# Attention of batches 2 to 4 inside a matmul stream: visits of three groups in place of two

## The chip, the cores and the metric

The kernel runs on one core of a Trainium2 chip. The metric is the device time of one execution in microseconds (us), the median of three timed runs. One more execution was profiled; it has a time and a trace of its own.

## What is computed

Windowed attention over four batches, then two feed-forward blocks over all 2304 tokens. In the reference, cut to what matters here:

```python
# q, k, v: (4, 8, 576, 64)
scores = scale * q @ k.T                       # 32 keys back; heads 4-7 with a stride of 4
scores = where(mask, scores, -1e9); scores -= max(scores)
attn = exp(scores); attn /= attn.sum() + 1e-9
x = (attn @ v).transpose(0, 2, 1, 3).reshape(2304, 512)
x = ((x @ w_a) * (x @ w_b)) @ w_out            # 512 -> 1536 -> 512
h = x @ w_in                                   # 512 -> 2048
out = (max(h, 0) + alpha * min(h, 0)) @ w_out2 # 2048 -> 512
```

## The kernel before

**The big matmuls.** Every large product is made of three matmuls of float32r data (high part times high, high times low, low times high). Tokens lie along the free axis. The first three token tiles, of 512 tokens each, take 37 **steps** each: for each of the 12 slices `f` of the hidden axis a step for product `pa`, a step for `pb`, and a step that expands the slice before into the four accumulators `accA` (lines 519 to 521), 12 matmuls of 128x512 in each step. Between them VectorE multiplies `g = pa*pb` (line 853, the "gate product") and ScalarE and VectorE split it into parts (line 282 and 279). After the third tile come the last 768 tokens and the second block, which the change doesn't touch in its code.

**Attention.** A **group** is two heads by three query windows of 64; a batch has 12 groups. Batch 1 is done ahead of the first tile. Batches 2, 3 and 4 are woven into tiles 1, 2 and 3, in **visits**. A group passes through these methods of `Group`:

- `scores` (line 378): six float32 matmuls of 64x64 by 96 columns. Each occupies a quarter of the array; the trace shows each float32 matmul as two records, so a group has 12.
- `largest` (393, VectorE): mask and row maximum, "maxima"; `exps` (407, ScalarE): three exponentials with their sums; `weigh` (414 to 418, VectorE): divides by the sums.
- `transposed` (430): three transposes through TensorE, one record each; `moved` (435, ScalarE): copies them out of PSUM as `pt`.
- `values` (443): six matmuls of 96x64 by 64 columns, 12 records; `placed` (477, VectorE): copies into the token tile.

A visit (`visit_scores`) issues the value products of the two groups of the visit before, and the scores of two new ones, ahead of one step's matmuls; `visit_turn` transposes both new groups together three steps later. A batch is 7 visits: the first has scores alone, the last values alone, five have both. The times of visits in steps come from `slots` (about 2.25, 2.64 and 2.3 steps a group in the three tiles).

**Order.** `at_step(before, k, fn)` and `at_step(after, k, fn)` hang work ahead of or behind the matmuls of step `k`; `behind` comes last in a step. What is not pinned by `keep_in_program_order` a scheduler may move by its own estimate of times. `convey` advances jobs that convert weights (read from `in_w2`, written to `wsd`). All DMAs go through SyncE's queue. `reload_o` fetches the output weights of slice `f` for tiles 2 and 3 (`wof`, `wod`). `load_qk(n + 3)` and `load_v(n + 3)` ask for the data of the group after next-but-one as soon as group `n` has used its place; there are three places for each.

Of the kernel before, what the change touches and what calls it, by code (L numbers as in the profile page):

```python
# [25 lines left out]
QT = 64  # L26
# [4 lines left out]
GS = 3  # L31
KS = GS * QT + WINDOW
# [33 lines left out]
def tile_kernel(ctx: ExitStack, tc: tile.TileContext, qk, v, mask, wab, wo1, w2, alpha, out):  # L66
# [57 lines left out]
    st_ring = Ring(ft, a0 + 2400, GS * KT, 2)  # L124
    et_ring = Ring(ft, a0 + 2976, GS * KT, 3)
    pt_ring = Ring(ft, a0 + 3840, GS * 2 * QT, 2)
    sm_ring = Ring(ft, a0 + 4608, 3 * GS, 4)
    mk = cut(ft, a0 + 4648, 720).bitcast(BF16).rearrange("p (m k) -> p m k", m=5)
# [13 lines left out]
    nal = cut(ft, a0 + 5376, NFB)  # L142
# [6 lines left out]
    held = [start_of[t] + x for t in (2, 3) for x in (-2, -1, 0, 1)]  # L149
# [199 lines left out]
    class Group:  # L349


        def __init__(self, b, i):
# [3 lines left out]
            self.swap = 0  # L356
            self.shared = None
# [5 lines left out]
        def scores(self):  # L363
            Group.scores_of([self])

        @staticmethod
        def scores_of(groups):


            for a, group in enumerate(groups):  # L370
                group.swap = a
                group.tq = tqs.pop(group.n)
                group.sp = group.psum(0, "sp") if group.shared is None else group.shared
            for s in range(GS):
                for group in groups:
                    for j in range(2):
                        half, to = (slice(x * 64, (x + 1) * 64) for x in (j, j ^ group.swap))
                        nc.tensor.matmul(
                            group.sp[to, s * KT:(s + 1) * KT],
                            lhsT=group.tq[half, s * QT:(s + 1) * QT],  # L380
                            rhs=group.tq[half, GS * QT + s * QT:GS * QT + s * QT + KT],
                            start=True, stop=True,
                        )
            for group in groups:
                if group.b:
                    at_step(after, now[0] + 1, lambda n=group.n + 3: behind.append(lambda: load_qk(n)))

        def largest(self, then=None):
            then = then.weights() if then else iter(())
            self.st = st_ring.next().rearrange("p (s k) -> p s k", k=KT)  # L390
            self.sm = sm_ring.next().rearrange("p (a s) -> p a s", s=GS)
            for s in range(GS):
                ins = nc.vector.tensor_tensor_reduce(  # L393
                    out=self.st[:, s], in0=self.sp[:, s * KT:(s + 1) * KT],
# [4 lines left out]
                if self.n in (NC * NG, NC * NG + 1) and s == 0:  # L399
# [4 lines left out]
        def exps(self):  # L404
            self.et = et_ring.next().rearrange("p (s k) -> p s k", k=KT)
            for s in range(GS):
                nc.scalar.activation(  # L407
                    self.et[:, s], self.st[:, s], AF.Exp, bias=self.sm[:, 0, s:s + 1], scale=-1.0, accum_out=self.sm[:, 1, s:s + 1]
                )
            self.st = None  # L410
# [27 lines left out]
        def values(self):  # L438
            tv = tvs.pop(self.n)
            self.ap = self.psum(2, "ap") if self.shared is None else self.shared[:, GS * KT:]  # L440
            for s in range(GS):
                for j in range(2):
                    nc.tensor.matmul(
                        self.ap[j * 64:(j + 1) * 64, s * QT:(s + 1) * QT],
                        lhsT=tv[:, s, j], rhs=self.pt[:, s, j ^ self.swap],
# [3 lines left out]
            if self.b:  # L449
                at_step(after, now[0] + 1, lambda n=self.n + 3: behind.append(lambda: load_v(n)))  # L450
# [819 lines left out]
```

## Time and profile before

| what | value |
|---|---|
| median of three runs | 865.87 us (865.82 to 866.27) |
| profiled execution, its own time | 865.0 us |
| its span in the trace | 863.2 us, 1.8 us less than its time |
| busy: TensorE, VectorE, ScalarE | 855.7, 626.7, 538.9 us |
| mean granted TensorE clock | 0.999 of full speed |

The span runs from the first to the last instruction of the trace. TensorE's busy time counts overlapping matmuls once; a matmul's own duration is longer than the distance to the next one, so costs are read from starts, not from durations. A visit is read from the start of the last large matmul ahead of it to the start of the second large matmul behind it.

### The profile page before, as it was taken

The numbers are of one execution on the slowest core, as the hardware profiler recorded it, in microseconds if no ns is written. First come the engines' busy times: TensorE is split into PE (matmuls) and PEld (weight loads), VectorE is DVE, ScalarE is ACT, GpSimd is POOL, SyncE is SP. The second block draws the span as 40 slices with busy tenths as digits, with TensorE's granted clock in tenths as the row PEclk, the third lists the DMA queues.
The fourth block names the chain that finished last, engine by engine and source line by source line (L and its number), as shares of the span: only waits on it lengthen the run. The fifth ranks groups of instructions, "written<-read, shape, count | busy, mean of one in ns | idle before, by whom it ended". The sixth has DMA issues, their size and how long they took to land.

```text
span 863.2 us, 15630 instructions
## 1 busy us (share of the span) xinstructions
PE 855.7 (99%) x5416; PEld 779.1 (90%) x5416; DVE 626.7 (73%) x1450; ACT 538.9 (62%) x1195; POOL 0.7 (0%) x6
## 2 busy tenths in 40 slices
PE   9999999999999999999999999999999999999998
PEld 5688887888878888899999999999999999999998
DVE  5788675567676678789796837997567896567954
ACT  7998874556655667655544537785566755665542
POOL 0000000000000000000000000000000000000000
PEclk9999999999999999999999999999999999999999
DMA  9999864589899898989555659788888887778875
GB/s 263 332 327 314 284 244 152 198 274 312 268 319 320 286 319 288 323 310 320 201 189 192 217 178 321 252 251 261 269 258 254 250 265 221 231 247 259 268 223 184
DMA packets 108126, 225.28 MB, mean 261 GB/s; under 512 B 12305, under 2 KB 27409, under 8 KB 108049
## 3 DMA queue, kind: packets, MB, share of 16 engines
q1 hardware_dynamic: 108048, 224.30, 79.2%
q8 instruction: 43, 0.70, 0.3%
q14 instruction: 35, 0.28, 0.1%
HBM read 169.72 MB, written 54.53 MB: 260 GB/s over the span
## 4 chain that ended last, share of the span: by engine, by line
PE 83%; DMA 8%; DVE 4%; ACT 4%; issue 1%; SPq 0%; ACTq 0%; DVEq 0%
PE acc L1179 20%; PE at L874 12%; PE pb L874 8%; PE pa L874 8%; DMA wsd<-rt 4%; PE accA L519 4%; PE accA L521 4%; PE accA L520 4%; PE pa L519 3%; PE pb L519 3%; PE pa L521 3%; PE pa L520 3%; PE pb L520 3%; PE pb L521 3%; DMA ft<-in_w 2%; PE tp L430 1%
## 5 line engine op out<-in xcount | busy, mean ns | idle before, releaser
L1179 PE MATMUL acc<-rt 128*128 128x384 f32 x1008 | 187.2, 334 | 0.0
L1179 PEld LDWEIGHTS acc<-rt 128*128 128x128 f32 x1008 | 175.8, 188 | 0.4 <-ACT ft L1162 0.4
L282 DVE TENSOR_TENSOR rt<-ft,rt 128x512 fp32r<-128x512 f32 (+3 forms) x165 | 116.3, 709 | 60.2 <-ACT rt L279 59.4
L279 ACT CAST rt<-ft 128x512 fp32r<-128x512 f32 (+3 forms) x165 | 103.6, 636 | 84.9 <-DMA wsd<-rt 20.4
L890 ACT COPY ft<-at 128x384 f32<-128x384 f32 x105 | 50.0, 476 | 53.6 <-PE at L874 52.6
L874 PE MATMUL at<-rt 128*128 128x384 f32 x414 | 83.4, 335 | 0.0
L874 PEld LDWEIGHTS at<-rt 128*128 128x128 f32 x414 | 72.6, 188 | 0.5 <-ACT ft L890 0.5
L519 PE MATMUL accA<-rt 128*128 128x512 f32 (+1 forms) x160 | 62.9, 393 | 0.2 <-ACT rt L279 0.2
L520 PE MATMUL accA<-rt 128*128 128x512 f32 (+1 forms) x160 | 61.7, 386 | 0.2 <-DVE rt L282 0.2
L521 PE MATMUL accA<-rt 128*128 128x512 f32 (+1 forms) x160 | 61.2, 385 | 0.1
L196 DVE SCALAR_TENSOR_TENSOR ft<-ft 128x512 uint32<-128x512 uint32 x60 | 41.2, 686 | 27.3 <-ACT ft L193 21.0
L407 ACT ACTIVATE ft<-ft 128x96 f32<-128x96 f32 x144 | 52.1, 365 | 12.0 <-DVE ft L393 11.9
L282 DVE TENSOR_TENSOR rt<-gx,rt 128x768 fp32r<-128x768 f32 x43 | 41.1, 956 | 21.5 <-ACT rt L279 21.1
L874 PE MATMUL pb<-rt 128*128 128x384 f32 x276 | 55.6, 336 | 0.0
L874 PE MATMUL pa<-rt 128*128 128x384 f32 x276 | 55.2, 334 | 0.0
L874 PEld LDWEIGHTS pb<-rt 128*128 128x128 f32 x276 | 48.3, 188 | 0.5
L279 ACT CAST rt<-gx 128x768 fp32r<-128x768 f32 x43 | 36.0, 836 | 20.4 <-PE acc L1179 18.8
L874 PEld LDWEIGHTS pa<-rt 128*128 128x128 f32 x276 | 48.5, 188 | 0.0
L193 ACT ACTIVATE ft<-ft 128x512 uint32<-128x512 uint32 x60 | 40.4, 673 | 12.3 <-DMA ft<-in_w 12.1
L190 ACT ACTIVATE ft<-ft 128x512 f32<-128x512 f32 x60 | 40.1, 670 | 10.9 <-DMA ft<-in_w 6.9
L874 PE MATMUL at<-rt,rx 128*128 128x384 f32 x216 | 43.9, 337 | 0.2 <-ACT ft L890 0.2
L874 PEld LDWEIGHTS at<-rt,rx 128*128 128x128 f32 x216 | 37.8, 188 | 1.2 <-ACT ft L890 1.2
(157 smaller groups left out, 1755.3 us busy)
## 6 DMA issues: line engine op xcount, KB each, us to landing
rt<-wsd SPq DMA_DIRECT2D x318, 256.0 KB, 3.2
wsd<-rt SPq DMA_DIRECT2D x112, 256.0 KB, 4.7
ft<-in_w SPq DMA_DIRECT2D x32, 512.0 KB, 5.8
ft<-in_qk SPq DMA_DIRECT2D x48, 208.0 KB, 5.0
ft<-in_wab SPq DMA_DIRECT2D x19, 512.0 KB, 6.4
rt<-wod SPq DMA_DIRECT2D x19, 512.0 KB, 5.1
rx<-wod SPq DMA_DIRECT2D x17, 512.0 KB, 4.5
ft<-in_v SPq DMA_DIRECT2D x48, 144.0 KB, 5.1
```

The source lines that it names most:

```text
L190: held(nc.scalar.activation(f, high.bitcast(F32), AF.Prelu, scale=2.0 ** -112, alpha=-2.0 ** 32))
L193: nc.scalar.activation(low, low, AF.Copy, scale=0.933 * 2.0 ** -29)
L196: nc.vector.scalar_tensor_tensor(out=fi, in0=fi, scalar=3, in1=low, op0=ALU.logical_shift_left, op1=ALU.bitwise_or)
L279: hi_eng.copy(hi, x)
L282: lo_eng.tensor_tensor(out=lo, in0=x, in1=hi.bitcast(F32), op=ALU.subtract)
L407: nc.scalar.activation(self.et[:, s], self.st[:, s], AF.Exp, bias=self.sm[:, 0, s:s + 1], scale=-1.0, accum_out=self.sm[:, 1, s:s + 1])
L519: nc.tensor.matmul(acc, lhsT=wh, rhs=rh, start=first, stop=False)
L520: nc.tensor.matmul(acc, lhsT=wh, rhs=rl, start=False, stop=False)
L521: nc.tensor.matmul(acc, lhsT=wl, rhs=rh, start=False, stop=last)
L874: nc.tensor.matmul(acc[:, :HT], lhsT=a, rhs=x[:, b, c], start=start and c == k == 0, stop=c == 1 and k == 2, skip_group_check=not start,)
L890: nc.scalar.copy(out, acc[:, :HT])
L1179: nc.tensor.matmul(acc[a][:, :HT], lhsT=u, rhs=q[:, b, i % 2], start=new and first and k == 0, stop=last and k == 2, skip_group_check=not new,
```

## The change

Visits of batches 2 to 4 now handle three groups (`VISIT`), so a batch has 5 visits, one every 6 steps, from step 8 of tile 1 and step 5 of tiles 2 and 3 (the scores of the very first stand three steps earlier). Each group is transposed alone, in steps 3, 4 and 5 behind its visit. Nine score windows alternate between two PSUM banks; the values of the groups go to the bank `pa`, which the product `pa` also uses, and the last window to the end of a score bank. Scores are kept in program order. Maxima and exponentials share their places, which leaves room for three `pt`. Maxima are queued behind all else of the visit's step, the gate product too. The loads of queries and keys follow in steps 1, 2 and 3 behind the visit, those of values in steps 2, 3 and 4. `reload_o` asks one step sooner and splits where it did. One more step, three ahead of tile 3, goes without `convey`.

```diff
 GS = 3
+VISIT, VISITS_AT = 3, (8, 5, 5)
...
-    st_ring = Ring(ft, a0 + 2400, GS * KT, 2)
-    et_ring = Ring(ft, a0 + 2976, GS * KT, 3)
-    pt_ring = Ring(ft, a0 + 3840, GS * 2 * QT, 2)
-    sm_ring = Ring(ft, a0 + 4608, 3 * GS, 4)
+    et_ring = Ring(ft, a0 + 2400, GS * KT, 4)
+    pt_ring = Ring(ft, a0 + 3552, GS * 2 * QT, 3)
+    sm_ring = Ring(ft, a0 + 4704, 3 * GS, 6)
...
-    held = [start_of[t] + x for t in (2, 3) for x in (-2, -1, 0, 1)]
+    held = [start_of[t] + x for t in (2, 3) for x in (-2, -1, 0, 1)] + [start_of[2] - 3]
...
-            at_step(after, k + 2, lambda: split(hi, lo, lo.bitcast(F32), nc.scalar, nc.vector))
-            at_step(after, k + 4, lambda: tc.keep_in_program_order(nc.sync.dma_start(out=wod[f], in_=w.bitcast(F32))))
+            at_step(after, k + 3, lambda: split(hi, lo, lo.bitcast(F32), nc.scalar, nc.vector))
+            at_step(after, k + 5, lambda: tc.keep_in_program_order(nc.sync.dma_start(out=wod[f], in_=w.bitcast(F32))))
...
-        def scores_of(groups):
-
-
-            for a, group in enumerate(groups):
-                group.swap = a
-                group.tq = tqs.pop(group.n)
-                group.sp = group.psum(0, "sp") if group.shared is None else group.shared
+            if not self.sp:
+                bank = self.psum(0, "sp")
+                self.sp = [bank[:, s * KT:(s + 1) * KT] for s in range(GS)]
+            tq = tqs.pop(self.n)
             for s in range(GS):
-                for group in groups:
-                    for j in range(2):
-                        half, to = (slice(x * 64, (x + 1) * 64) for x in (j, j ^ group.swap))
-                        nc.tensor.matmul(
-                            group.sp[to, s * KT:(s + 1) * KT],
-                            lhsT=group.tq[half, s * QT:(s + 1) * QT],
-                            rhs=group.tq[half, GS * QT + s * QT:GS * QT + s * QT + KT],
-                            start=True, stop=True,
-                        )
-            for group in groups:
-                if group.b:
-                    at_step(after, now[0] + 1, lambda n=group.n + 3: behind.append(lambda: load_qk(n)))
+                for j in range(2):
+                    half, to = (slice(x * 64, (x + 1) * 64) for x in (j, j ^ self.swap[s]))
+                    ins = nc.tensor.matmul(
+                        self.sp[s][to], lhsT=tq[half, s * QT:(s + 1) * QT],
+                        rhs=tq[half, GS * QT + s * QT:GS * QT + s * QT + KT], start=True, stop=True,
+                    )
+                    if self.b:
+                        tc.keep_in_program_order(ins)
+            if self.b:
+                at_step(after, now[0] + 1 + self.n % VISIT, lambda n=self.n + 3: behind.append(lambda: load_qk(n)))
 
...
-            self.st = st_ring.next().rearrange("p (s k) -> p s k", k=KT)
+            self.et = et_ring.next().rearrange("p (s k) -> p s k", k=KT)
             self.sm = sm_ring.next().rearrange("p (a s) -> p a s", s=GS)
             for s in range(GS):
                 ins = nc.vector.tensor_tensor_reduce(
-                    out=self.st[:, s], in0=self.sp[:, s * KT:(s + 1) * KT],
+                    out=self.et[:, s], in0=self.sp[s],
...
-            self.et = et_ring.next().rearrange("p (s k) -> p s k", k=KT)
             for s in range(GS):
                 nc.scalar.activation(
-                    self.et[:, s], self.st[:, s], AF.Exp, bias=self.sm[:, 0, s:s + 1], scale=-1.0, accum_out=self.sm[:, 1, s:s + 1]
+                    self.et[:, s], self.et[:, s], AF.Exp, bias=self.sm[:, 0, s:s + 1], scale=-1.0, accum_out=self.sm[:, 1, s:s + 1]
...
-            self.ap = self.psum(2, "ap") if self.shared is None else self.shared[:, GS * KT:]
+            if not self.ap:
+                self.ap = [(0, self.psum(2, "ap"))]
             for s in range(GS):
+                o, ap = max((x for x in self.ap if x[0] <= s), key=lambda x: x[0])
                 for j in range(2):
                     nc.tensor.matmul(
-                        self.ap[j * 64:(j + 1) * 64, s * QT:(s + 1) * QT],
-                        lhsT=tv[:, s, j], rhs=self.pt[:, s, j ^ self.swap],
+                        ap[j * 64:(j + 1) * 64, (s - o) * QT:(s - o + 1) * QT],
+                        lhsT=tv[:, s, j], rhs=self.pt[:, s, j ^ self.swap[s]],
                         start=True, stop=True,
                     )
             self.pt = None
             if self.b:
-                at_step(after, now[0] + 1, lambda n=self.n + 3: behind.append(lambda: load_v(n)))
+                at_step(after, now[0] + 2 + self.n % VISIT, lambda n=self.n + 3: behind.append(lambda: load_v(n)))
...
     def visit_scores(k, new, old):
 
-        shared = []
-
         def products():
-            while len(shared) < 2:
-                shared.append(bank_at(f"sa{k}_{len(shared)}"))
-            for group, bank in zip(old, shared):
-                group.shared = bank
+            even, odd, both = bank_at(f"se{k}"), bank_at(f"so{k}"), bank("pa")
+            for a, group in enumerate(old):
+                n = GS * QT * a
+                group.ap = [(0, both[:, n:])]
+                if a == VISIT - 1:
+                    group.ap.append((2, odd[:, 4 * KT:]))
                 group.values()
-            for group, bank in zip(new, shared):
-                group.shared = bank
-            if new:
-                Group.scores_of(new)
-
+            for a, group in enumerate(new):
+                at = range(GS * a, GS * a + GS)
+                group.swap = [u % 2 for u in at]
+                group.sp = [(even, odd)[u % 2][:, u // 2 * KT:(u // 2 + 1) * KT] for u in at]
+                group.scores()
+
+        def then(k, *fns):
+            at_step(before, k, lambda: [at_step(after, k, fn) for fn in fns])
+
+        rest = 3 if new and new[0].n == NC * NG else 0
         at_step(before, k, products)
-        first = int(bool(new) and new[0].n == NC * NG)
-        for group in new:
-            at_step(after, k + first, group.largest)
-        for group in old:
-            at_step(after, k, group.placed)
-        for group in new:
-            at_step(after, k + 1 + first, group.exps)
-            at_step(after, k + 1 + first, group.weigh)
-
-    def visit_turn(k, mid):
-
-        for group in mid:
-            group.tags = [("at", 2)] * 3
-            at_step(before, k, group.transposed)
-            at_step(after, k, group.moved)
+        then(k, *[group.placed for group in old])
+        then(k + rest, *[group.largest for group in new])
+        then(k + rest + 1, *[fn for group in new for fn in (group.exps, group.weigh)])
+
+    def visit_turn(k, group):
+
+        group.tags = [("at", 2)] * 3
+        at_step(before, k, group.transposed)
+        at_step(after, k, group.moved)
...
     for t in range(1, N_PLAIN):
         for f in range(NFA):
-            reload_o(start_of[t] + 3 * f, t, f)
+            reload_o(start_of[t] + 3 * f - 1, t, f)
     for t in range(3):
-        slots = [start_of[t] + (7 if t == 0 else 0) + int(j * (2.25, 2.64, 2.3)[t]) for j in range(NC * NG)]
         groups = [Group(t + 1, i) for i in range(NC * NG)]
-        pairs = [groups[j:j + 2] for j in range(0, NC * NG, 2)]
-        for j in range(len(pairs) + 1):
-            k = slots[2 * j] if j < len(pairs) else slots[-1] + 2
-            visit_scores(k, pairs[j] if j < len(pairs) else [], pairs[j - 1] if j else [])
-            if j < len(pairs):
-                visit_turn(k + 3, pairs[j])
+        sets = [groups[j:j + VISIT] for j in range(0, NC * NG, VISIT)]
+        for j in range(len(sets) + 1):
+            k = start_of[t] + VISITS_AT[t] + 6 * j
+            visit_scores(k if t or j else k - 3, sets[j] if j < len(sets) else [], sets[j - 1] if j else [])
+            for a in range(VISIT if j < len(sets) else 0):
+                visit_turn(k + 3 + a, sets[j][a])
```

**TensorE, batch 4, the visit in which groups 6 to 8 have their value products.** Before, the pair 6 and 7 (`sa109`: two banks that hold scores and values), between an expansion and the next `pa`; "x6" counts float32 matmuls:

```order
L521 MATMUL accA2_3_2925<-rt_70 128x512
L443 MATMUL sa109_0_3332<-ft_72 64x64 x6
L443 MATMUL sa109_1_3333<-ft_72 64x64 x6
L378 MATMUL sa109_0_3332<-ft_72 64x96 x2
L378 MATMUL sa109_1_3333<-ft_72 64x96 x2
L378 MATMUL sa109_0_3332<-ft_72 64x96 x2
L378 MATMUL sa109_1_3333<-ft_72 64x96 x2
L378 MATMUL sa109_0_3332<-ft_72 64x96 x2
L378 MATMUL sa109_1_3333<-ft_72 64x96 x2
L519 MATMUL pa_3331<-rt_70,rx_878 128x512
```

In the changed program (line 435 is now the value product, 371 the score, 512 to 514 the large matmul; `se114` and `so114` are the score banks):

```order
L435 MATMUL pa_3461<-ft_72 64x64 x6
L512 MATMUL accA2_0_2848<-rt_70 128x512
...
L435 MATMUL pa_3461<-ft_72 64x64 x6
L513 MATMUL accA2_3_2851<-rt_70 128x512
...
L435 MATMUL pa_3461<-ft_72 64x64 x4
L435 MATMUL so114_3460<-ft_72 64x64 x2
L371 MATMUL se114_3459<-ft_72 64x96 x2
...
L371 MATMUL se114_3459<-ft_72 64x96 x2
L512 MATMUL pa_3534<-rt_70,rx_849 128x512
```

The scheduler has put 10 large matmuls between the value products of the first and second group and 11 between the second and third, so this visit is entered three times. The whole of tiles 1 to 3, counted in both orders (an entry is a stretch of attention matmuls with large matmuls on both sides):

| entries | tile 1 | tile 2 | tile 3 | all |
|---|---|---|---|---|
| before: transposes | 6 | 6 | 6 | 18 |
| before: visits | 8 (one in two pieces) | 7 | 8 (one in two pieces) | 23 |
| changed: transposes | 12 | 12 | 12 | 36 |
| changed: visits | 5 | 10 (3, 3 and 2 pieces in the last three) | 10 (2, 3 and 3 pieces in the last three) | 25 |

**TensorE, batch 2, a middle visit of the changed program.** The value products of its three groups (16 matmuls in `pa`, 2 in `so31`) and its nine score windows stand in one stretch; the expansion follows:

```order
L435 MATMUL pa_881<-ft_72 64x64 x16
L435 MATMUL so31_880<-ft_72 64x64 x2
L371 MATMUL se31_879<-ft_72 64x96 x2
...
L371 MATMUL se31_879<-ft_72 64x96 x2
L512 MATMUL accA0_0_619<-rt_70 128x512
```

All of tile 1, and the first two visits of the other tiles, stand like this.

**SyncE, batch 4, loads of values (`in_v`) of the last groups.** Before, the two loads of a visit stand together, behind a reload of output weights (`wod`) and a weight job:

```order
L324 DMA rt_70<-wod_64 128x1024
L203 DMA wsd_67<-rt_70 128x512 x2
L208 DMA ft_72<-in_w2 128x512 x2
L347 DMA ft_72<-in_v 96x384 x2
L342 DMA ft_72<-in_qk 128x416
```

In the changed program they stand apart, the first ahead of the reload and the others behind it:

```order
L347 DMA ft_72<-in_v 96x384
L324 DMA rt_70<-wod_64 128x1024
L203 DMA wsd_67<-rt_70 128x512 x2
L347 DMA ft_72<-in_v 96x384
L203 DMA wsd_67<-rt_70 128x512 x2
L347 DMA ft_72<-in_v 96x384
```

The load of the third group moved behind two pairs of stores of converted weights and a reload that waits for an expansion on TensorE.

## Rows read from the trace of the kernel before

**Rows 1.** Page: busy time of TensorE and its share of the span

```profile
PE 855.7 (99%) x5416; PEld 779.1 (90%) x5416; DVE 626.7 (73%) x1450; ACT 538.9 (62%) x1195; POOL 0.7 (0%) x6
```

**Rows 2.** TensorE timeline, visit of two groups: start, length, line, tiles, count

```profile
59.06 0.39 PE L521 MATMUL pb<-rt 128*128 128x512 f32 x1
59.38 0.92 PE L443 MATMUL sa<-ft 96*64 96x64 f32 x24
60.22 0.73 PE L378 MATMUL sa<-ft 64*64 64x96 f32 x24
60.88 0.50 PE L519 MATMUL accA<-rt 128*128 128x512 f32 x1
61.22 0.39 PE L520 MATMUL accA<-rt 128*128 128x512 f32 x1
61.45 0.40 PE L521 MATMUL accA<-rt 128*128 128x512 f32 x1
```

**Rows 3.** TensorE timeline: the transposes of two groups

```profile
55.66 0.39 PE L521 MATMUL pa<-rt 128*128 128x512 f32 x1
55.89 0.82 PE L430 MATMUL tp<-ident,ft 128*96 128x128 f32 x6
56.47 0.48 PE L519 MATMUL pb<-rt 128*128 128x512 f32 x1
56.78 0.40 PE L520 MATMUL pb<-rt 128*128 128x512 f32 x1
```

**Rows 4.** TensorE timeline: a visit with value products alone

```profile
131.24 0.92 PE L443 MATMUL sa<-ft 96*64 96x64 f32 x24
132.09 0.50 PE L519 MATMUL pa<-rt 128*128 128x512 f32 x1
```

**Rows 5.** TensorE timeline: a visit with scores alone

```profile
143.34 0.73 PE L378 MATMUL sa<-ft 64*64 64x96 f32 x24
144.00 0.50 PE L519 MATMUL pa<-rt 128*128 128x512 f32 x1
```

**Rows 6.** TensorE timeline: eight score matmuls alone

```profile
46.94 0.39 PE L521 MATMUL pa<-rt 128*128 128x512 f32 x1
47.26 0.40 PE L378 MATMUL sa<-ft 64*64 64x96 f32 x8
47.58 0.50 PE L519 MATMUL pb<-rt 128*128 128x512 f32 x1
```

**Rows 7.** TensorE timeline, batch 1: value products of one group

```profile
9.50 0.57 PE L443 MATMUL ap<-ft 96*64 96x64 f32 x12
10.00 0.39 PE L611 MATMUL pb<-zeros 128*128 128x512 bf16 x1
```

**Rows 8.** Last visit: TensorE timeline, SyncE timeline, loads of in_v (three views)

```profile
341.06 1.16 PE L443 MATMUL sa<-ft 96*64 96x64 f32 x24
...
336.17 0.43 SPq L347 DMA_DIRECT2D ft<-in_v  x1
...
DMA to landing us min/median/max: 2.2/5.1/7.8
```

**Rows 9.** SyncE timeline: loads of in_v beside the visit of rows 2

```profile
59.98 0.81 SPq L347 DMA_DIRECT2D ft<-in_v  x2
```

**Rows 10.** TensorE timeline: scores of batch 4 that stand in two pieces

```profile
253.20 0.38 PE L378 MATMUL sa<-ft 64*64 64x96 f32 x2
253.81 0.50 PE L519 MATMUL accA<-rt 128*128 128x512 f32 x1 [0.23 <-ACT rt L279]
```

**Rows 11.** VectorE timeline: first and last of six maxima, batch 4

```profile
286.67 0.25 DVE L393 CUSTOM_DVE_ANT_0 ft<-sa,ft 128x96 f32<-128x96 f32 x1
...
287.56 0.26 DVE L393 CUSTOM_DVE_ANT_0 ft<-sa,ft 128x96 f32<-128x96 f32 x1
```

**Rows 12.** ScalarE timeline: first and last of six exponentials, batch 4

```profile
286.97 0.38 ACT L407 ACTIVATE ft<-ft 128x96 f32<-128x96 f32 x1 [1.05 <-DVE ft L393]
...
288.78 0.36 ACT L407 ACTIVATE ft<-ft 128x96 f32<-128x96 f32 x1
```

More of the change, by code (lines that the diff above doesn't have):

```diff
@@ L123, in tile_kernel @@
     v_ring.places.insert(0, v_ring.places.pop())
-    st_ring = Ring(ft, a0 + 2400, GS * KT, 2)
-    et_ring = Ring(ft, a0 + 2976, GS * KT, 3)
-    pt_ring = Ring(ft, a0 + 3840, GS * 2 * QT, 2)
-    sm_ring = Ring(ft, a0 + 4608, 3 * GS, 4)
-    mk = cut(ft, a0 + 4648, 720).bitcast(BF16).rearrange("p (m k) -> p m k", m=5)
+    et_ring = Ring(ft, a0 + 2400, GS * KT, 4)
+    pt_ring = Ring(ft, a0 + 3552, GS * 2 * QT, 3)
+    sm_ring = Ring(ft, a0 + 4704, 3 * GS, 6)
+    mk = cut(ft, a0 + 4760, 720).bitcast(BF16).rearrange("p (m k) -> p m k", m=5)
     xn_pair = cut(ft, 4096, 4, 2 * HT)
@@ L141, in tile_kernel @@
     s_places = [cut(ft, 10752 + HT * i, HT) for i in range(3)]
-    nal = cut(ft, a0 + 5376, NFB)
+    nal = cut(ft, a0 + 5480, NFB)
     n_start = NC * NG + 5
@@ L355, in __init__ @@
             self.tags = [("at", 2), ("acc%d" % (3 * (i % 2)), 1), ("acc%d" % (1 + i % 2), 1)]
-            self.swap = 0
-            self.shared = None
+            self.swap = [0] * GS
+            self.sp, self.ap = [], []
         def psum(self, n, what):
@@ L398, in largest @@
                 )
-                if self.n in (NC * NG, NC * NG + 1) and s == 0:
+                if NC * NG <= self.n < NC * NG + VISIT and s == 0:
                     tc.keep_in_program_order(ins)
@@ L404, in exps @@
         def exps(self):
-            self.et = et_ring.next().rearrange("p (s k) -> p s k", k=KT)
             for s in range(GS):
                 nc.scalar.activation(
-                    self.et[:, s], self.st[:, s], AF.Exp, bias=self.sm[:, 0, s:s + 1], scale=-1.0, accum_out=self.sm[:, 1, s:s + 1]
+                    self.et[:, s], self.et[:, s], AF.Exp, bias=self.sm[:, 0, s:s + 1], scale=-1.0, accum_out=self.sm[:, 1, s:s + 1]
                 )
-            self.st = None
         def weights(self):
@@ L463, in placed @@
                     p = e
-            rest = []
+            rest, firsts = [], [(first * QT, bank) for first, bank in self.ap]
             for o, n, t0, hop in segs:
                 while n:
+                    o0, bank = max((x for x in firsts if x[0] <= o), key=lambda x: x[0])
+                    end = min([x for x, _ in firsts if x > o], default=GS * QT)
                     t = max(i for i, (first, _) in enumerate(TILES) if first <= t0)
-                    k = min(n, (TILES[t][0] + TILES[t][1] - t0 + hop - 1) // hop)
+                    k = min(n, end - o, (TILES[t][0] + TILES[t][1] - t0 + hop - 1) // hop)
                     c0 = t0 - TILES[t][0]
-                    to, x = (slice(None), self.pr, slice(c0, c0 + (k - 1) * hop + 1, hop)), self.ap[:, o:o + k]
+                    to, x = (slice(None), self.pr, slice(c0, c0 + (k - 1) * hop + 1, hop)), bank[:, o - o0:o - o0 + k]
                     if not t:
```

2 lines of the change are left out of this document (removed).

## The prediction

> **What bounds the kernel now.** I read the page first: TensorE is busy for 855.7 us [rows 1] of a span of 863.2, so time is won or lost by what TensorE has to do, or by making it wait. That share is of overlapping matmuls and cannot show what a visit costs. The second view is therefore TensorE's timeline around one visit of each kind, read by starts. Inside a step one large matmul follows another after 0.23 us (61.22 to 61.45) [rows 2]. Whatever is longer between two starts is the price of what stands between them.
>
> Around a whole visit the last large matmul ahead starts at 59.06 and the second behind at 61.22; less two ordinary distances (0.46) the visit costs 1.70 us [rows 2]. The reader should see where it lies: 0.09 more than usual to get in (59.06 to 59.38), 0.84 for 24 records of values, 0.66 for 24 of scores, 0.11 more than usual to get out (60.88 to 61.22). Transposes are different: into them the distance is the ordinary 0.23, and six cost 56.78 - 55.66 - 0.46 = 0.66, or 0.11 each, with nothing left over for the entry [rows 3].
>
> Values alone cost 0.09 + 0.85 + 0.11 = 1.05 [rows 2, 4], scores alone 0.09 + 0.66 + 0.11 = 0.86 [rows 5]. Twelve records of values take 0.50 [rows 7] where 24 take 0.85, so twelve more cost 0.35 and a stretch of values has a fixed part of 1.05 - 0.70 = 0.35. Eight scores cost 0.09 + 0.32 + 0.11 = 0.52 [rows 6] where 24 cost 0.86: 0.085 for each four, the number that fill the four quarters of the array at once, and 0.35 fixed. So an extra entry into scores or values costs 0.35, an extra entry into transposes nothing.
>
> **The attention matmuls before, in the three tiles.** 18 pairs of groups' transposes at 0.66 are 11.88; 15 whole visits at 1.70 are 25.5; 3 with values alone 3.15; 3 with scores alone 2.58; two of these stand in two pieces, 0.70. Two waits can be read: 0.24 in the last visit, whose 24 records last 1.16 and not 0.92 [rows 8], and 0.23 behind the scores at 253.20, where an expansion waits for a split of output weights [rows 10]. Together 44.28 us.
>
> **The same after the change.** A whole visit has 12 more records of values (+0.35) and 12 more of scores. Nine windows alternate between quarters as six did; eight of them make full fours, the ninth has no partner. I take four more slots of 0.085, +0.34, which makes 2.39. With no partner at no cost it would be three slots; over 12 visits with scores that bound is 1.0 us lower. First visits cost 0.86 + 0.34 = 1.20, last ones 1.05 + 0.35 = 1.40.
>
> - 9 whole visits: 21.51; 3 first: 3.60; 3 last: 4.20.
> - 36 transposes of one group: no row has three transposes between large matmuls. By the row of six they are 0.33 each, together 11.88. If a part of the 0.66 were fixed, as large as that of values, three would take (0.66 - 0.35)/2 + 0.35 = 0.505, together +6.3 us. The row is the same operation with the same neighbours and shows an entry of the ordinary distance, so I take 0.33.
> - The order of the changed program has 25 entries of visits and not 15, ten of them extra. At 0.35 that is 3.50. From below an entry could cost what transposes pay, nothing: -3.5. The rows of values and scores themselves give 0.35, so I take it.
>
> The sum is 44.69, that is 0.4 more than before. The saving of merging seven visits into five (44.28 less 41.19, about 3 us) is given back by the pieces in which six visits of tiles 2 and 3 stand.
>
> A rule of the Trainium skill speaks to the entries: its page TensorEngine Tiling (Key Properties) says that changing the tiling mode, not just the tile, drains TensorE. The trace agrees for scores and values, 0.35, and shows nothing of it for transposes. Applied to every entry, 20 more than before, the rule would make entries alone cost some 7 us more than before; by the rows it is 0.7, for the net two entries of visits.
>
> **Other parts, and what covers them.** *Maxima and exponentials.* Six maxima are 0.18 apart (286.67 to 287.56 is five distances) [rows 11], six exponentials 0.36 (286.97 to 288.78) [rows 12]. Nine take 1.6 and 3.3. Before, both groups' transposes came three steps, 36 large matmuls, behind the scores; now the first group's do, the others a step (2.8 us) later each, which covers them. Least cover: the visit of batch 4 shown in the order has 19 large matmuls, 4.4 us, ahead of the first transposes, and these need three exponentials, not nine. Without cover the first group would wait up to 3.3 - 1.1 = 2.2. Nothing. *The gate product ahead of the maxima, the moved places, one step without `convey`*: VectorE is idle for 27% of the span [rows 1]; nothing on TensorE's path. *The bank `pa`*: a visit stands ahead of an expansion, so its copies have the scores (1 us) and 12 matmuls (2.8) before `pa` is written again. In the visit shown, `pa` follows right behind the scores, but there only the last group's copies are still open. Nothing, up to 0.5 in that visit. *Output weights a step sooner*: takes the 0.23 of [rows 10], counted as a wait of before; the split stands where it stood. *Loads*: no byte more. The third group's values are asked for two steps ahead of their visit, where before all had at least four. Waits for these and for the rest I put at 0.2, less than the 0.47 of before, since most late products stand behind large matmuls that TensorE has; the bounds are nothing and the second rival.
>
> **Sum.** 44.69 + 0.2 - 44.28 = +0.6 us. The profiled execution's own time is 865.0, so 865.6; the median of the runs shown lies 0.87 above it, and times are compared with that: 865.87 + 0.6 = **866.5 us**. About 0.2%, 1.7 us, is what a measurement of this kernel can tell from no change, so "no change" is 864.1 to 867.6.
>
> **The rivals.**
>
> *Values land late (slower).* Loads of `in_v` take 2.2 to 7.8 us, median 5.1 [rows 8]. If SyncE issues the third group's only at the end of the step that asks, then in an unbroken visit its products are due after one step (2.8), a group's transposes (0.33), the entry (0.09) and two groups of values (0.70): 3.9 us. At the median each of three middle visits of batch 2 waits 1.2, 3.6 in all; the third tile, where the load of [rows 8] took 5.3 (336.17 to about 341.5) and already delayed values, has the large matmuls between the pieces ahead of them (21 of them, 4.8 us, in the visit shown) and waits little. Without the 0.2 that is 866.3 + 3.6 = 869.9. For it: the 0.24 of before, and a queue in which the load stands behind others. Against: in batch 2 SyncE issued the loads at 59.98, right behind the values at 59.38 [rows 2, 9], ahead of its program by more than a step. It decides from 3.9 us between step end and landing.
>
> *Every entry pays (slower).* If the 0.35 holds for transposes as well: 866.5 + 6.3 = 872.8. Against it stands the row of six.
>
> *The pieces are cheap (faster).* If large matmuls between values overlap the change of mode, so that an extra entry costs nothing, as it does for transposes, and the ninth window finds room: 866.5 - 3.5 - 1.0 = 862.0; with half of it 864.2. For it: part of the edges overlaps already. Against: eight scores alone paid the full 0.35 [rows 6].
>
> *The change doesn't do what it says* is excluded where visits stand whole; where they stand in pieces it is the forecast.
>
> **How the numbers follow.** Forecast 0.56; late values 0.24; every entry pays 0.06; cheap pieces 0.14. The predicted time is the forecast's 866.5. Half of the cheap case lies under 864.2 and the late case is at 869.9, so 864.3 to 869.9 leaves out about 2 in 10 with the case of 872.8. Within 0.2% are the forecast without its upper edge and part of the cheap case; faster 0.12, same 0.56, slower 0.32.
>
> **What would show it.** Timeline: a whole visit costs 2.39, a single group's transposes 0.33, a piece of six value products 0.70. Total of attention in the three tiles: 44.7. Values that wait would show as a stretch longer than 36 records need, with a landing of `in_v` just ahead; late weights as transposes with idle time ended by VectorE. The prediction is wrong if pieces cost well under 0.35, if transposes pay for their entry, or if waits for `in_v` sum to over 1.5 us.

## The result: about 1% slower, and the profile after

The changed kernel takes 874.79 us (median of 6 runs, 873.26 to 878.53) against 866.5 for the kernel before in the same series (6 runs): a ratio of 1.0104, interval 1.008 to 1.0128. The forecast was 866.5. The profiled execution took 874.44, its span is 872.6.

The page of the changed kernel: span, busy time [rows 1], and the first line of the chain that ended last.

```profile
span 872.6 us, 15591 instructions
PE 859.0 (98%) x5416; PEld 778.3 (89%) x5416; DVE 629.8 (72%) x1462; ACT 539.0 (62%) x1195; POOL 0.7 (0%) x6
...
PE 84%; DMA 8%; DVE 4%; ACT 1%; issue 1%; SPq 1%; ACTq 0%; DVEq 0%
```

TensorE is busy 3.3 us longer in a span that is 9.4 us longer, so two thirds of the loss are idle time. The chain's share of DMAs says nothing on it, for it is 8% in the kernel before too. So the prices come first, then the waits.

TensorE's timeline of the changed kernel answers to [rows 2] and [rows 3]. It shows the transposes of one group, a whole visit, and the second piece of a visit of batch 3 (line 420 is the transpose, 435 the value product, 371 the score).

```profile
163.10 0.39 PE L514 MATMUL pb<-rt 128*128 128x512 f32 x1
163.33 0.49 PE L420 MATMUL tp<-ident,ft 128*96 128x128 f32 x3
...
163.89 0.39 PE L513 MATMUL accA<-rt 128*128 128x512 f32 x1
...
172.38 0.39 PE L514 MATMUL pb<-rt 128*128 128x512 f32 x1
172.69 1.15 PE L435 MATMUL pa<-ft 96*64 96x64 f32 x32
...
175.20 0.40 PE L513 MATMUL accA<-rt 128*128 128x512 f32 x1
...
193.36 0.40 PE L513 MATMUL accA<-rt 128*128 128x512 f32 x1
194.75 0.57 PE L435 MATMUL pa<-ft 96*64 96x64 f32 x12 [0.99 <-DMA ft<-in_v]
...
195.59 0.39 PE L512 MATMUL accA<-rt 128*128 128x512 f32 x1
```

Read as in the prediction, by starts and less two ordinary distances, three transposes cost 163.89 - 163.10 - 0.46 = 0.33, a whole visit 175.20 - 172.38 - 0.46 = 2.36 (2.37 to 2.39 by the unrounded times of five such visits). The prices are right. The piece of six value products at 194.75 costs 195.59 - 193.36 - 0.46 = 1.77, where 0.70 was forecast, and the row names why: 0.99 of idle time, ended by the load of `in_v`.

The waits of TensorE in the changed kernel, longest sums first (us in total, times, longest):

```profile
PE pa L435 <- DMA ft<-in_v: 3.8, 5, 1.2
PE accA L512 <- ACT rt L279: 1.8, 2, 1.2
```

The waits of SyncE's queue that concern the output weights (line 326 loads from `wof` for tile 2, 324 from `wod` for tile 3; "DMA wod<-rt" is the store that still reads the place, "PE accA" the expansion that does):

```profile
SPq L326 <- DMA wod<-rt: 35.1, 9, 7.0
...
SPq L324 <- PE accA L514: 22.2, 6, 6.4
SPq L326 <- PE accA L514: 21.3, 5, 10.4
```

In the kernel before, the first of these waits was a third as long:

```profile
SPq L326 <- PE accA L521: 25.6, 5, 11.3
SPq L326 <- DMA wod<-rt: 12.0, 5, 3.8
```

With the smaller lines of the same view, SyncE stood 60.6 us ahead of loads from `wof`, and 39.7 before.

How such a wait can reach TensorE is read at the piece above. SyncE's timeline of the changed kernel:

```profile
183.96 0.51 SPq L342 DMA_DIRECT2D ft<-in_qk  x1
189.33 0.33 SPq L326 DMA_DIRECT2D rt<-wof  x1
189.75 0.85 SPq L203 DMA_DIRECT2D wsd<-rt  x2
190.66 0.45 SPq L347 DMA_DIRECT2D ft<-in_v  x1
```

and the chain of the stretch from 186 to 196, in order of time (start, us, what):

```profile
189.53 0.13 SPq L326
...
190.66 4.05 DMA ft<-in_v
...
194.75 0.57 PE pa L435 x12
```

From 184.5 to 189.33 SyncE issues nothing: it stands before a load of output weights, 4.8 us for the store and then 0.2 for TensorE. Two stores and the load of `in_v` stand behind it in the queue; when that is issued at 190.66, its 4.05 us to landing are no longer covered.

This is the only place in tiles 2 and 3 at which the chain that ended last passes through a load of output weights. At the next piece that waits, at 217.51, such a load stood 2.7 us too, but the chain's last releaser ahead of `in_v` is VectorE, which the store between them waits for:

```profile
211.97 0.44 DVE ft L271
212.40 0.19 SPq L203
...
212.65 4.82 DMA ft<-in_v
```

The same holds for the longest wait of an expansion, at the turn to tile 3. SyncE's timeline, the chain, then ScalarE's timeline and TensorE's:

```profile
244.56 0.45 SPq L347 DMA_DIRECT2D ft<-in_v  x1
248.99 0.32 SPq L326 DMA_DIRECT2D rt<-wof  x1
```

```profile
248.79 0.61 DVE rt L282
...
249.43 0.36 SPq L203
...
250.30 6.82 DMA ft<-in_w
```

```profile
257.14 0.65 ACT L193 ACTIVATE ft<-ft 128x512 uint32<-128x512 uint32 x1 [1.72 <-DMA ft<-in_w]
257.70 0.60 ACT L279 CAST rt<-ft 128x512 fp32r<-128x512 f32 x1
```

```profile
258.35 1.20 PE L512 MATMUL accA<-rt 128*128 128x512 f32 x4 [1.23 <-ACT rt L279]
```

SyncE stands 4 us before the load of `wof` here. But the two stores behind it became ready only at 249.40, when VectorE had finished their data, so with VectorE's times as they are `in_w` would hardly have been issued sooner without the load. It lands 6.82 us after its issue; ScalarE, in order, waits for it, and the split that the expansion needs is behind that.

Of the three waits for values in batch 4 (1.6 us together) two lie on the chain, and there too VectorE comes ahead of their loads. All three loads took 6.5 to 8.0 us to landing, as this one, issued behind two loads of `in_w`:

```profile
308.84 7.79 DMA ft<-in_v
...
316.77 0.24 PE pa L435
```

The 9.4 us in sum, by starts over the same stretch of both traces (38 to 362 us): attention 49.9 against 44.9, +5.0; large matmuls between, +3.0, half of it at 258; behind the tiles, stalls of the last stages, +1.1; the rest lies ahead of the tiles. Without the waits that are in it the attention is 44.8 us, where 44.7 was forecast. (The same reading gives 44.9 for the kernel before, where the prediction's sum was 44.28, so the agreement holds to about half a us.) That is, pieces and prices came out as worked out; the loss is waits.

### The profile page after: what moved, and what is told of

It is laid out like the page before. It is cut to its first block, busy times and chain, and to the rows that moved or that the text cites. A ratio compares the mean times of both kernels' runs of the same rounds, so it can differ in the third digit from the quotient of the medians.

```text
span 872.6 us, 15591 instructions
## 1 busy us (share of the span) xinstructions
PE 859.0 (98%) x5416; PEld 778.3 (89%) x5416; DVE 629.8 (72%) x1462; ACT 539.0 (62%) x1195; POOL 0.7 (0%) x6
## 4 chain that ended last, share of the span: by engine, by line
PE 84%; DMA 8%; DVE 4%; ACT 1%; issue 1%; SPq 1%; ACTq 0%; DVEq 0%
PE acc L1171 20%; PE at L866 11%; PE pb L866 7%; PE pa L866 7%; PE accA L512 4%; DMA ft<-in_v 4%; PE accA L514 4%; PE accA L513 3%; PE pa L514 3%; PE pa L513 3%; PE pa L512 3%; PE pb L512 3%; PE pb L513 3%; PE pb L514 3%; DMA ft<-in_w 2%; DMA wsd<-rt 1%
## 5 line engine op out<-in xcount | busy, mean ns | idle before, releaser
L512 PE MATMUL accA<-rt 128*128 128x512 f32 (+1 forms) x160 | 64.1, 406 | 1.8 <-ACT rt L279 1.8
L513 PE MATMUL accA<-rt 128*128 128x512 f32 (+1 forms) x160 | 62.2, 388 | 0.0
L514 PE MATMUL accA<-rt 128*128 128x512 f32 (+1 forms) x160 | 62.0, 388 | 0.0
L282 DVE TENSOR_TENSOR rt<-gx,rt 128x768 fp32r<-128x768 f32 x43 | 41.1, 956 | 21.5 <-ACT rt L279 21.1
```

Of the source, the lines that this page charges most:

```text
L282: lo_eng.tensor_tensor(out=lo, in0=x, in1=hi.bitcast(F32), op=ALU.subtract)
L512: nc.tensor.matmul(acc, lhsT=wh, rhs=rh, start=first, stop=False)
L513: nc.tensor.matmul(acc, lhsT=wh, rhs=rl, start=False, stop=False)
L514: nc.tensor.matmul(acc, lhsT=wl, rhs=rh, start=False, stop=last)
```

## The experiments

Three causes were set against each other: loads of values that are asked for too late by their own schedule; the earlier loads of output weights, which would hold what is behind them on SyncE's queue (the theory); and the step without `convey`, which crowds the steps beside it. Each run has one or a few edits against the changed kernel, unless said otherwise; ratios are to the kernel before, with intervals.

### Values asked for soon

```diff
-at_step(after, now[0] + 2 + self.n % VISIT, lambda n=self.n + 3: behind.append(lambda: load_v(n)))
+at_step(after, now[0] + 1, lambda n=self.n + 3: behind.append(lambda: load_v(n)))
```

> The changed kernel, but the values of all three groups are asked for one step behind the visit, as before, and not in steps 2, 3 and 4. Theory L (values land late): the waits for in_v (some 5 us in the three tiles) go, and with them the pieces, since the order of this program has one extra entry in place of ten (3.2 us): about 866.5 us. Rival D (the DMA engines are full, and when a load is asked for matters little): waits of 3 us or more for in_v stay, 870 or more. Rival C (the loss is from weight jobs moved by the step without conversion): the time stays within 2 us of the changed kernel, 873 or more.

872.89 us, ratio 1.0078 (1.0052 to 1.0103). The waits for `in_v` are gone, but others stand in their place; the two largest of TensorE:

```profile
PE se L371 <- DMA ft<-in_qk: 2.8, 3, 1.4
PE accA L512 <- ACT rt L279: 2.3, 2, 1.9
```

SyncE still stands 37.6 us, ten times, before loads of `wof` that wait for a store to `wod`. Only some 2 us come back, and the 866.5 of theory L was missed: the load that comes late is now another one.

### Output weights asked for when they were before

```diff
-            reload_o(start_of[t] + 3 * f - 1, t, f)
+            reload_o(start_of[t] + 3 * f, t, f)
-            at_step(after, k + 3, lambda: split(...))
-            at_step(after, k + 5, lambda: ...dma_start(out=wod[f], ...))
+            at_step(after, k + 2, lambda: split(...))
+            at_step(after, k + 4, lambda: ...dma_start(out=wod[f], ...))
```

> The changed kernel, but the output weights are asked for where they were asked for before, one step later. Theory L in its second form (a load of values stands in SyncE's queue behind a load of output weights that waits for an expansion on TensorE): the values asked for in steps 3 and 4 are issued sooner, waits for in_v fall from 5 us to under 2 and the order has four extra entries in place of ten (2.1 us less): about 869 us. If only the steps in which values are asked for matter: waits for in_v stay at 4 us or more, 872. Rival C: 873 or more.

867.01 us, ratio 1.0016 (0.9996 to 1.0035): no measurable difference to before. This one edit was worth 7.8 us. TensorE's waits for `in_v` fall to 1.5. SyncE's waits for the store to `wod` fall to 13.8 us, about what they were before; those for the expansion are longer than in the changed kernel (21.3):

```profile
SPq L326 <- PE accA L514: 30.5, 7, 10.4
SPq L326 <- DMA wod<-rt: 13.8, 6, 6.3
```

The order has four extra entries here and not ten, so part of the gain (up to 2.1 by 0.35 each) is that; the time is 2 us below the expected 869. The expansion near 258 doesn't wait any more.

### Both

> Both: values of all three groups asked for one step behind the visit, output weights as before. The order has no extra entry. Theory L: attention in the three tiles costs 41.3 us by the prices of the prediction and no wait for in_v over 0.3: about 863.5 us, faster than before by 3. Rival D: waits of 3 us or more stay, 867 or more. Rival C: at least 2.5 us are lost at the end of tiles 2 and 3, 866 or more.

867.42 us, ratio 1.0007 (0.999 to 1.0024). No visit stands in pieces and the attention takes 41.2 us, 3.3 less than with the weights alone put back; but large matmuls around it wait 3.3 more (1.18 of it at 236.97 for copies out of `pa`, 1.42 at 254.81 for a split on ScalarE behind `in_w`). So the price of the merging came out, and the expected 863.5 did not. SyncE's wait for the store is 21.4 us here, although the weights are asked for as before.

### The step without convey taken away

```diff
-    held = [...] + [start_of[2] - 3]
+    held = [...]
```

> The changed kernel with the step three ahead of tile 3 given back to the weight jobs. Rival C: the wait of 1.4 us at the end of tile 2 and about 1 us around the end of tile 3 go, 872 us or less. Theory L: the visits of tiles 2 and 3 stay in pieces (eleven extra entries in this order) and wait for in_v as they do, 873 to 876.

875.68 us, ratio 1.0094 (1.0062 to 1.0127), as the change: by the median that cause falls. Its one run at a mean granted clock of 1.000 took 870.88, the other three, at 0.996 to 0.998, over 875; the changed kernel's four at 1.000 took 873.26 to 875.14. So a gain of some 3 us that the lower clock hides is not excluded.

### The whole chain of output weights a step sooner

The split and the store to `wod` are put one step sooner too, so that the next load has the store's old lead.

> The changed kernel, but the split and the store of the output weights move one step sooner with their load, so that the store to wod has two steps again before its place is loaded anew. Theory S (SyncE's queue stands at the load of output weights until that store has landed, 35.1 us in nine waits in the changed kernel, none in w_back, and the loads of values and queries behind it come late): these waits fall under 10 us, waits for in_v under 2.5 us, time 866 to 869, although the order still stands in pieces (nine or ten extra entries). Rival E (the load waits for the expansion that frees its place, which asking a step sooner makes longer): nothing of that is taken away, 872 or more.

873.74 us, ratio 1.0073 (1.0046 to 1.01). SyncE's wait for the store falls by more than half, but not the time: more of it now stands before the expansion on TensorE that still reads the place.

```profile
SPq L326 <- PE accA L514: 33.0, 7, 10.4
SPq L326 <- DMA wod<-rt: 16.2, 7, 6.8
```

TensorE waits 3.2 us for `in_v`, little less than in the changed kernel. So the store alone is not the cause: in sum SyncE stands 58.9 us ahead of these loads, against 60.6. The expectation is wrong where it says that the kernel with the weights as before had no wait for the store; it had 13.8.

### The kernel before with that one edit

> The kernel before with one edit alone: output weights asked for a step sooner, split and stored where they were. Theory S: SyncE waits for the store to wod as in the changed kernel, 30 us or more, but visits of two groups ask for values four steps ahead or more, so TensorE loses 1 to 5 us: 868 to 871. Rival (only the visits of three groups make the loss): 866.5, within 1 us of before. Rival E: as theory S in time, but SyncE waits for expansions and not for the store.

870.99 us, ratio 1.0054 (1.0032 to 1.0075): in visits of two groups, too, the edit alone costs some 4.5 us. The attention has 41 entries as in the kernel before, so no new pieces are in it. SyncE's wait for the store grows from 12.0 to 33.4 us, and the chain of the stretch from 244 to 258 shows the same place as above:

```profile
246.80 0.66 DVE ft L196
...
248.26 5.79 DMA ft<-in_w
...
255.30 0.52 ACT rt L279
...
255.86 1.19 PE accA L519 x4
```

Here too the last to release what stands ahead of `in_w` is VectorE.

### Values soon, weights as before, no extra step without convey

> Values asked for one step behind the visit, output weights as before, and the step three ahead of tile 3 given back to the weight jobs. No visit stands in pieces. If that step is what makes ScalarE late at the end of tile 2 (1.4 us in v_soon_w_back) and VectorE late with the copies out of pa (1.2 us): both go, 865 or less, under before. If late weight data for the conversion is the cause wherever the step lies: 866 to 868, as v_soon_w_back.

865.65 us, ratio 0.9993 (0.9979 to 1.0007), between the two ranges of the expectation. Attention 41.7; one expansion waits 1.96 at 256.01, for ScalarE behind `in_w` again, so the extra step was not what made ScalarE late.

### Maxima ahead of the gate product again

```diff
-        then(k, *[group.placed for group in old])
-        then(k + rest, *[group.largest for group in new])
+        for group in new:
+            at_step(after, k + rest, group.largest)
+        for group in old:
+            at_step(after, k, group.placed)
```

with the output weights as before.

> Output weights as before, and the maxima of a visit queued ahead of the copies and of the gate product, as in the kernel before. Cost of the order on VectorE: if the gate product matters, expansions wait for ScalarE's split of it by 1 us or more in tiles 1 to 3, or pa waits for copies; if not, 865 to 868 with no such wait, as w_back.

One run, 871.38 us. It doesn't decide on the order: waits for `in_v` (4.1 us, two of them) hide what it does. No expansion waited for the gate product. What it does show is the granted clock behind its two long waits, in windows behind the one of 2.01 us that ends at 236.97 and the one of 2.07 that ends at 314.74 (us, busy time of PE, PEld, DVE, ACT, POOL with counts, granted clock, DMA share, GB/s):

```profile
238.50:242.30 3.80, 3.80 (x11) 2.99 (x10) 2.47 (x10) 1.07 (x3) 0.00 (x0) 0.55 0.62 177
242.30:250.00 7.70, 7.70 (x36) 6.33 (x35) 4.55 (x7) 3.97 (x7) 0.00 (x0) 1.00 0.95 334
...
315.00:319.00 4.00, 4.00 (x59) 3.31 (x55) 3.78 (x25) 2.85 (x10) 0.00 (x0) 1.00 0.27 65
```

### Output weights on GpSimd's queue

```diff
-nc.sync.dma_start(out=..., in_=wod[f] / wof[f])
+nc.gpsimd.dma_start(out=..., in_=wod[f] / wof[f])
```

This was to part two readings of the second cause: Q, what is queued behind the waiting load costs; T, asking so soon costs in itself. It was run in the changed kernel, in two of the variants above, and in the kernel before.

> The changed kernel with one difference: the loads of output weights are issued from GpSimd's own queue and not from SyncE's. They are asked for at the same step and wait for the same store and expansion, but nothing else stands behind them. In the order of the instructions no visit stands in pieces any more, which alone takes 3.5 us from the changed kernel's 874.8. Theory Q (what costs the time is what is queued on SyncE behind a load that waits): the waits for in_v and for in_w behind them go, attention in the tiles sums to 41.5 to 43, and the time is 864 to 867.5. Rival T (the time of asking itself, or the weights landing late): the waits stay, attention sums to 44 or more, and the time is 870 to 872.

> The changed kernel with the loads of output weights on GpSimd's queue and the loads of all three groups' values asked for one step behind the visit, not two to four. Theory Q: with nothing held on SyncE's queue the later asking for values costs little, so this is within 1.5 us of the same kernel with values asked for as in the change; 863 to 866.5. Rival V (the values' own later asking costs even in a free queue): 2 us or more faster than it.

> Visits of three groups with four edits: output weights asked for when they were before, and on GpSimd's queue; values asked for one step behind the visit; no extra step without converting. Its twin with the output weights on SyncE's queue took 865.65. Theory Q: in that one SyncE's queue still stood 19 us behind loads of output weights that wait for an expansion; without that the expansion that waited 1.96 near 256 and the stalls of 0.4 go, and the time is 862.5 to 864.5. Rival T: no difference, 865 to 866.5.

> The kernel before (visits of two groups) with the loads of output weights on GpSimd's queue. SyncE stood 25.6 us behind such loads in the kernel before, and TensorE's waits that lead back to late loads sum to about 1 us there. Theory Q: 864.5 to 866, since little hung on that queue. Rival T: no change. Above 868: GpSimd's queue itself is slower.

893.99, 894.46, 890.3 and 890.48 us, ratios 1.028 to 1.033: the ranges of Q and of its rivals missed by over 20 us in all four. For the kernel before the expectation had a third reading, GpSimd's queue itself is slower, whose range (above 868) holds 890.48; it is not parted from the new order either. The order shows no pieces, and TensorE's list has no wait for `in_v` any more, as Q has it. But the order on the other engines is another one, and new waits are far larger. Those of TensorE in the changed kernel with this edit:

```profile
PE pa L435 <- ACT ft L841: 10.6, 6, 3.3
PE accA L512 <- ACT rt L279: 6.4, 2, 3.9
```

ScalarE's timeline ahead of the longest of the first kind (line 841 copies `pa`):

```profile
241.76 0.62 ACT L279 CAST rt<-rt 128x512 fp32r<-128x512 f32 x1 [2.60 <-DMA rt<-wof]
242.29 0.58 ACT L841 COPY ft<-pa 128x512 f32<-128x512 f32 x1
```

The scheduler has put the split of the output weights ahead of the copy that frees `pa`, and the weights landed late (issued at 233.72, landed at 241.74); now ScalarE's order holds the copy. The mean granted clock of the four profiled executions is lower too, 0.984 to 0.990; by an estimate from this and their spans of 891 to 895 us, at most 9 to 14 us of each are the clock's. As a test between Q and T it is void.

### The loads last in their step

```diff
-        at_step(after, k, load)
+        at_step(after, k, lambda: behind.append(load))
```

> The changed kernel with one difference: the loads of output weights are asked for in the same step as in the change, but as the last thing of the step and not among its first. Loads of values and queries of the same step come ahead of them on SyncE's queue; those of the next steps still stand behind. Theory Q (what is queued behind a load that waits is what costs): part of the loss comes back, 870 to 873.5, and waits for in_v are under 3 us. Rival T (asking for output weights that soon costs in itself, by the places or the traffic): 874 to 876, as the change.

871.71 us, ratio 1.0067 (1.004 to 1.0093). Some 3 us come back with no change of step, and SyncE's wait for the store to `wod` falls from 35.1 us to 21.1. TensorE still waits for `in_v`:

```profile
PE pa L435 <- DMA ft<-in_v: 2.4, 3, 1.4
PE pa L435 <- ACT rt L279: 2.0, 1, 2.0
```

That is Q's result, in its range and outside T's. But its interval overlaps that of the change a little, and its visits stand in five extra pieces and not ten, which by 0.35 each is up to 1.75 of the 3 us. One wait for `in_v`, 1.37 us at 194.95, again stands behind a load that waits for the store. So the run speaks for Q without closing the question.

### Input weights three steps ahead

The kernel of 865.65 with `lead=3` in place of 2 in `convert_s`.

> The kernel with values asked for soon, output weights as before and no extra step without converting, which took 865.65, with one more edit: input weights of the second block are loaded three steps ahead of their first use in tiles 1 to 3, not two. There an expansion near 256 waited 1.96 us for ScalarE, which waited for in_w (6.2 us to landing). Theory W (late in_w is what is left): that wait goes and the time is 863 to 865. Rival: the loads only move the crowd on the queue, 865 to 867.

865.23 us, ratio 0.998 (0.9968 to 0.9991); the interval overlaps that of the kernel of 865.65, so the lead is not shown to gain. The stall of 1.96 is 0.86, at 254.17, and VectorE ends it; attention takes 41.3. The wait shrank as theory W has it, but the time is in the rival's range, 0.2 us outside the theory's. The same lead in the kernel before wasn't tried, so the 0.2% is not shown to come from visits of three groups.

### How long SyncE stands ahead of the loads from `wof`

For the kernels that issue these loads on SyncE's queue, the sums of all lines `SPq L326` in the list of its waits, and the part that the store ended:

| kernel | median, us | SyncE stands, us | for the store, us |
|---|---|---|---|
| before | 866.5 | 39.7 | 12.0 |
| before, weights a step sooner | 871.0 | 50.3 | 33.4 |
| values soon, weights as before, no extra step, `lead=3` | 865.2 | 43.7 | 16.3 |
| values soon, weights as before, no extra step | 865.7 | 44.4 | 19.3 |
| values soon, weights as before | 867.4 | 47.6 | 21.4 |
| weights as before | 867.0 | 51.4 | 13.8 |
| maxima first, weights as before (one run) | 871.4 | 53.1 | 14.4 |
| loads last in their step | 871.7 | 54.0 | 21.1 |
| whole chain a step sooner | 873.7 | 58.9 | 16.2 |
| values soon | 872.9 | 60.4 | 37.6 |
| changed | 874.8 | 60.6 | 35.1 |
| step without `convey` taken away | 875.7 | 61.5 | 34.1 |

Among the kernels with visits of three groups the time rises nearly in the order of the whole sum, and not with the store's part. That goes with the theory, but a slower TensorE also frees the places later, and each sum is of one execution. The kernel before with the edit is slower than the one with weights as before, at about the same sum, so what stands behind the load matters too.

## Why the prediction was wrong, step by step

- **Prices of visits, transposes and pieces**: right. 0.33, 2.37 and 0.70 where nothing waits; 44.8 us in all without waits against 44.7. The rivals *every entry pays* (35 of the 36 transposes at 0.334 to 0.344 each, one waits) and *the pieces are cheap* fall. The rule of the Trainium skill (TensorEngine Tiling, Key Properties) that a change of tiling mode drains TensorE agrees with the trace after for scores and values (0.70 for a piece, 0.35 of it fixed). The transposes show nothing of it, and no run shows whether they change the mode at all.
- **"Output weights a step sooner: takes the 0.23 of [rows 10]"**: this step failed: a term that took 0.23 off cost several us. It priced the data's arrival and not the load's stand in the queue. A place of the two is read by the store to `wod` in step 3f+4 and was loaded anew in step 3f+6; the change makes that 3f+5, one step of 2.8 us for a store whose median to landing was 5.6 us around there (in tiles 2 and 3 of before). So the load waits for it longer (35.1 us in nine times, 12.0 in five before), and with it everything behind it on SyncE. Moving the store along hardly helped (873.74), since the expansion then holds the load. Put back, the edit gives 7.8 us in the changed kernel; alone it costs 4.5 us in the kernel before. That it is this edit is shown by both; the way to TensorE is shown for one wait of 0.99 us, at 194.75. The order ahead of the prediction shows a reload between two loads of values that stood together; nothing was priced for it.
- **"Loads: waits 0.2"**: 5.1 us in the attention by starts; 3.8 us are idle time that `in_v` ended, which is over the 1.5 that the prediction named as its own sign of being wrong. The lead was counted from the step that asks and not from the issue on SyncE; for the 0.99 at 194.75 that is the same omission.
- **Rival *values land late***: right in kind, wrong in place. It looked in batch 2, where no visit waits; in that tile there are no reloads. Late are batches 3 (2.2 us) and 4 (1.6), and the pieces there do not cover them. In batch 4 its own reason holds, landings of 6.5 to 8.0 us; that its 3.6 us is near the measured 3.8 is luck.
- **Gate product, maxima, `pa`**: 0.2 us of waits for copies out of `pa` in the changed kernel, inside the 0 to 0.5 that was set. Without pieces they grew to 1.0.
- **One step without `convey`**: nothing by the medians, as forecast; some 3 us are not excluded, as said above.

What stays open: how the 7.8 us part into the held loads, the extra pieces that the scheduler makes with the edit, and the time of asking itself. That the held load carries the wait at 194.75 is shown in the rows. Ahead of the waits at 217.51 and 258.35 the chain names VectorE, and in batch 4 long landings; how the edit makes these longer is not shown.

## What to carry to other kernels

Before a load is moved ahead, ask what it must wait for at its new place and list what stands behind it on the same queue: all of them can pay the wait. With two places in a ring, a load that follows a store out of its place sooner than the store lands waits for it (here 35.1 us in place of 12.0). When a wait behind such a load is found, read the chain: here it named the load once and another releaser elsewhere. A load's lead is counted from its issue in the queue's order, not from the step that asks for it.

## What was not expected of the hardware

- The granted clock fell to 0.55 for 3.8 us shortly after TensorE had waited 2.01 us, that is to about the lower of its two levels (1.2 of 2.4 GHz). The 11 matmuls recorded in that stretch take 2.5 us at 0.23 each, so the wait of 2.01 was followed by a loss of some 1.3 more. It doesn't always follow: behind the wait of 2.07 us in the same trace the granted clock stayed at 1.00.
- Loads on GpSimd's queue: 0.54 us for an issue, where SyncE's took 0.32, and medians of 5.3 (`wof`) and 6.4 us (`wod`) to landing, where the same loads of the changed kernel have 3.0 and 4.4. The Trainium skill (DMA: Bandwidth & Descriptors, SWDGE vs HWDGE vs iDMA) calls that path slower to set up; these rows agree. How much of the 20 us that is, no run shows.
